# w_down as one DMA on 128 partitions and a fill tile ahead of the ring, in a decode kernel of cached attention and a gated feed-forward

## The chip, the cores and the metric

The kernel runs on one core of a Trainium2 chip. The metric is the device time of one execution in microseconds (us), the median of several runs; less is better.

## The reference

One token `x` of width 512 goes through two branches, and a scalar gate mixes them:

```python
g = sigmoid((x * gate_w).sum(-1, keepdims=True))
# a: attention of one query per head over a cache of 65536 keys; 32 heads of width 128
q = (x @ wq).reshape(B, Sq, H, Dh).transpose(0, 2, 1, 3)
scores = einsum("bhqd,bhkd->bhqk", q, k_cache) * Dh ** -0.5
o = einsum("bhqk,bhkd->bhqd", softmax(scores), v_cache)
a = o.transpose(0, 2, 1, 3).reshape(B, Sq, H * Dh) @ wo
# b: feed-forward of inner width 1792
b = (silu(x @ w_gate) * (x @ w_up)) @ w_down
out = g * a + (1 - g) * b
```

All tensors are bfloat16. K and V together are 1,073,741,824 bytes; w_down (1792 x 512) is 1,835,008 bytes, all other weights together some 12 MB.

## The kernel before

**Tiles and slots.** A head's K is cut into four tiles (`G = 4`), and so is its V, 128 tiles of each. A tile is 128 partitions x 128 rows x 128 bfloat16: 32,768 bytes in each partition, 4 MB, one DMA. The tiles live in a ring of five slots (`ring`, `SLOTS = 5`). `take` hands out the slot that has been free longest and `give` returns one; in the beginning the slots also hold the rest of wq (`wq_t`), w_gate and w_up (`gu_t`) and w_down (`wd_t`), and at the end the last half of wo (`wo_late`). Small tiles that stay for the whole kernel lie in `consts`, which is placed ahead of the ring in SBUF.

K0, K1, ... and V0, V1, ... below are the tiles by the number `n` of the code: K4 is K's fifth tile, the first of the second head.

**A tile of K.** VectorE multiplies it in place by the head's query (`products`, L254), then halves its width by adding (L258, once for the first head, twice after it). TensorE sums what is left over the width with an identity matrix (`scores`, L267), and VectorE adds up the last four columns (`fold`, L281). When a head's four tiles are through, the maximum and the exponentials follow (`row_max`, `exponentials`), and the weights of the sum go into `P_sb`.

**A tile of V.** TensorE multiplies it by the weights (`values`, L322, 32 matmuls a tile). V runs four tiles or more behind K. At the end of a head its result is turned, scaled and projected through wo (`head_copy`, `head_turn`, `project`).

**The order.** The program is scheduled by hand (`manual_schedule`): each engine runs its instructions in the order in which the code issues them. All large loads are issued by SyncE, in one queue. An issue waits until its slot has been released by the engine that read it last, and the issues behind it wait with it. Eight semaphores are used in turn for the DMAs, so that an issue also waits until the DMA eight places before it has landed.

**The beginning.** The order of the large loads is: the first columns of wq, K0, K1, K2, the rest of wq, w_gate, K3, w_up, then six DMAs of w_down (`load_wd`, L402), K4, two more of w_down, V0, K5, V1, K6, a piece of wo, V2, and so on in turns of V and K (L110). w_down takes the slot that K1 gives up, K4 the one of wq, V0 the one of K2, K5 the one of w_gate and w_up, V1 the one of K3, and K6 the one of w_down.

**w_down.** It lies on 64 partitions, 28 of its rows in each (`HP = 64`, `GT = 28`). Each of its eight DMAs fills eight partitions, every fourth one from a first partition on:

```python
firsts = (0, 1, 2, 3, 32, 33, 34, 35)
part = slice(firsts[i], firsts[i] + 29, 4)
nc.sync.dma_start(out=wd_sb[part], in_=wd_rows[part])
```

**The feed-forward branch.** `feed_forward_in` makes gate and up on 128 partitions, 14 values in each (L178), while the fourth tile of K is worked on. `feed_forward_mid` makes `hT`, 128 x 14, on VectorE in the step of K4, between its maximum and its second half. `feed_forward_out` follows on TensorE in the same step, ahead of V0's products: two small matmuls turn `hT` into 64 partitions x 28 (`h_ps`, L227), ScalarE copies them to `h2` (L231), 28 matmuls against w_down add up to `b_ps` (L233), ScalarE scales the result into `b_sb` (L236), and it opens the accumulators `a_ps` of the output (L238). Then w_down's slot is given back.

Of the kernel before, what the change touches and what calls it, by code (L numbers as in the profile page):

```python
# [8 lines left out]
ACT = mybir.ActivationFunctionType  # L9
ALU = mybir.AluOpType  # L10
AXIS = mybir.AxisListType
P = 128
# [21 lines left out]
def kernel(  # L34
# [14 lines left out]
    nc = tc.nc  # L49
    bf16 = mybir.dt.bfloat16  # L50
    f32 = mybir.dt.float32

    _, H, Sk, Dh = A_k_cache.shape
    D = A_x.shape[2]
    F = B_w_gate.shape[1]
    KT = D // P
    FT = F // P
# [7 lines left out]
    consts = ctx.enter_context(tc.tile_pool(name="consts", bufs=1))  # L65
# [7 lines left out]
    psum_m = ctx.enter_context(tc.tile_pool(name="psum_m", bufs=2, space=bass.MemoryType.PSUM))  # L73
# [7 lines left out]
    def take(name):  # L81
        slot = free.pop(0)
        held[name] = slot
        return ring.tile(
            [P, NB * Dh], bf16, name=name.split(".")[0], tag=f"slot{slot}"
        )

    def give(name):
        free.append(held.pop(name))

    xT = consts.tile([P, KT], bf16, name="xT")
    gwT = consts.tile([P, KT], bf16, name="gwT")
    with nc.allow_non_contiguous_dma(reason="small"):
# [19 lines left out]
    def load_k(n):  # L113
        load(K_tiles, A_k_cache, n, "K_t")
# [13 lines left out]
    ident_b = consts.tile([P, P], bf16, name="ident_b")  # L128
# [85 lines left out]
    def feed_forward_mid(gu_sb, eg):  # L214
        nc.vector.tensor_scalar_add(eg, eg, 1.0)
        nc.vector.reciprocal(eg, eg)
        hprod = consts.tile([P, FT], f32, name="hprod")
        nc.vector.tensor_tensor(out=hprod, in0=gu_sb[:, :FT], in1=eg, op=ALU.mult)
        hT = consts.tile([P, FT], bf16, name="hT")
        nc.vector.tensor_tensor(out=hT, in0=hprod, in1=gu_sb[:, FT:], op=ALU.mult)  # L220
        return hT

    def feed_forward_out(hT, rest):
        b_ps = psum_m.tile([1, D], f32, name="b_ps", tag="misc")
        h_ps = psum_m.tile([HP, GT], f32, name="h_ps", tag="misc")
        for r in range(2):
            nc.tensor.matmul(  # L227
                h_ps[:, r * FT : (r + 1) * FT], lhsT=ident_b[:, r::2], rhs=hT, start=True, stop=True
            )
        h2 = consts.tile([HP, GT], bf16, name="h2")  # L230
        nc.scalar.activation(out=h2, in_=h_ps, func=ACT.Copy)  # L231
        for t in range(GT):
            nc.tensor.matmul(  # L233
                b_ps, lhsT=h2[:, t : t + 1], rhs=wd_sb[:, t, :], start=(t == 0), stop=(t == GT - 1)
            )
        nc.scalar.activation(out=b_sb, in_=b_ps, func=ACT.Copy, scale=rest)  # L236
        for i, a in enumerate(a_ps):
            nc.tensor.matmul(  # L238
                a, lhsT=ones_f[0:1, 0:1], rhs=b_sb[:, i * HD : (i + 1) * HD], start=True, stop=False
            )  # L240
# [22 lines left out]
    def scores(n):  # L263
        S = F_tiles[n] = psum_s.tile([P, NB, QUAD], f32, name="S_ps")
        width = width_of(n)
        for c in range(0, width, QUAD):
            nc.tensor.matmul(  # L267
                S,
                lhsT=ident_b,
                rhs=K_tiles[n][:, :, c : c + QUAD],  # L270
                start=(c == 0),
                stop=(c == width - QUAD),
            )
        del K_tiles[n]
        give(f"K_t.{n}")
# [98 lines left out]
    def score_tile(n):  # L374
        for _ in products(n):
            pass
        if n:
            fold(n - 1)
# [11 lines left out]
    score_tile(1)  # L390
    xs = gate_sum()
    scores(1)
    wd_t = take("wd_t.0")
    HP = P // 2
    GT = F // HP
    wd_sb = wd_t[:HP, : GT * D].rearrange("p (t n) -> p t n", t=GT)
    wd_rows = B_w_down.rearrange("(p t) n -> p t n", t=GT)
    firsts = (0, 1, 2, 3, 32, 33, 34, 35)

    def load_wd(i):  # L400
        part = slice(firsts[i], firsts[i] + 29, 4)
        nc.sync.dma_start(out=wd_sb[part], in_=wd_rows[part])  # L402

    for i in range(6):
        load_wd(i)
    for g in range(1, H // QG):
        queries(g)
    give("wq_t.0")
    eg2 = gate_exp(xs)
    load_k(4)  # L410
    load_wd(6)
    load_wd(7)
    score_tile(2)
    rest = gate_value(eg2)
    scores(2)
# [17 lines left out]
    for n, v in steps:  # L433
# [22 lines left out]
        if n == G:  # L456
            hT = feed_forward_mid(*ff)
# [7 lines left out]
        if n == G:  # L465
            feed_forward_out(hT, rest)
            give("wd_t.0")
# [49 lines left out]
```

## Time and profile before

| | us |
|---|---|
| median of 3 runs | 2534.05 |
| lowest, highest run | 2532.77, 2534.06 |
| the profiled execution, its own time | 2534.41 |
| its span (first to last instruction) | 2532.6 |

| engine | busy us | share of the span |
|---|---|---|
| PE (TensorE matmuls) | 1533.7 | 61% |
| PEld (TensorE weight loads, beside the matmuls) | 581.6 | 23% |
| DVE (VectorE) | 2083.7 | 82% |
| ACT (ScalarE) | 77.7 | 3% |
| POOL (GpSimd) | 0.9 | 0% |

The profile is one execution. 1088.49 MB were moved by sixteen DMA engines, 430 GB/s over the span. In the profile's views PE, DVE, ACT, POOL and SP are the engines, a q behind the name is the engine's own queue in which it issues DMAs, L254 is line 254 of the kernel, and `out<-in` names the tile written and the tiles read. The chain of waits is followed back from the last instruction to whatever released each step. In the windows, a DMA's packet counts in the stretch in which it starts, so that shares of short stretches can be over 1.

### The profile page before, as it was taken

To read this page: it belongs to the slowest core of one execution; us is meant where nothing else is said; L and a number is where in the kernel's file an instruction comes from. 1 tells how busy PE (TensorE), PEld (TensorE's weight loads), DVE (VectorE), ACT (ScalarE), POOL (GpSimd) and SP (SyncE) were. 2 spreads that over 40 slices of the span, in tenths; PEclk is the share of its full clock that TensorE was granted. 3 is DMA by queue.
4 is the path that set the end of the run, shared out by engine and by line. 5 is a ranking of instruction groups with operands and counts; after the bars stand their busy time and mean duration, and the time that the engine had idled before them with its cause. 6 is when DMAs were issued, how large, how long until landed. Compare 5 with 4: busy or idle time off the path is not lost.

```text
span 2532.6 us, 13195 instructions
## 1 busy us (share of the span) xinstructions
PE 1533.7 (61%) x5786; PEld 581.6 (23%) x5786; DVE 2083.7 (82%) x744; ACT 77.7 (3%) x208; POOL 0.9 (0%) x7
## 2 busy tenths in 40 slices
PE   4656656665566555555665566556656665665569
PEld 1222222222222112222222122222222221222223
DVE  7788888888887999988888888888888888888860
ACT  1000000000000000000000000000000000000000
POOL 0000000000000000000000000000000000000000
PEclk9777777777777787787777777777777777777779
DMA  9999999999999999999999999999999999999998
GB/s 412 418 431 433 435 432 430 434 433 432 431 433 434 431 433 434 432 431 434 433 432 433 434 432 432 435 431 432 432 434 432 431 435 433 431 434 433 432 432 351
DMA packets 43915, 1088.49 MB, mean 430 GB/s; under 512 B 4753, under 2 KB 9362, under 8 KB 10258
## 3 DMA queue, kind: packets, MB, share of 16 engines
q1 hardware_dynamic: 43570, 1087.65, 99.7%
q8 instruction: 45, 0.74, 0.1%
q14 instruction: 12, 0.10, 0.0%
q10 hardware_dynamic: 288, 0.00, 0.0%
HBM read 1087.64 MB, written 0.00 MB: 429 GB/s over the span
## 4 chain that ended last, share of the span: by engine, by line
DMA 71%; PE 23%; DVE 4%; issue 1%; ACT 0%; SPq 0%; DVEq 0%
DMA V_t<-in_A_v_cache_dram 63%; PE O_ps L322 21%; DMA K_t<-in_A_k_cache_dram 8%; DVE K_t L254 3%; DVE K_t L258 1%; PE S_ps L267 1%; DMA wo_late<-in_A_wo_dram 0%; PE b_ps L233 0%; DVE S_sb L281 0%; DVE m L287 0%; PE oh_ps L351 0%; PE a_ps L238 0%; ACT P_sb L300 0%; PE a_ps L365 0%; PE mT_ps L291 0%
## 5 line engine op out<-in xcount | busy, mean ns | idle before, releaser
L322 PE MATMUL O_ps<-V_t,P_sb 128*4 128x512 bf16 x4094 | 1154.5, 452 | 663.5 <-DMA V_t<-in_A_v_cache_dram 663.5
L254 DVE TENSOR_TENSOR K_t<-K_t,q_bc 128x16384 bf16<-128x16384 bf16 (+1 forms) x159 | 1117.2, 7026 | 357.9 <-DMA K_t<-in_A_k_cache_dram 346.7
L258 DVE TENSOR_TENSOR K_t<-K_t 128x8192 bf16<-128x8192 bf16 (+1 forms) x314 | 859.7, 2738 | 8.6
L322 PEld LDWEIGHTS <-P_sb 128*4 128x4 bf16 x4094 | 393.0, 97 | 1405.1 <-issue 1064.1
L267 PE MATMUL S_ps<-K_t,ident_b 128*128 128x512 bf16 x1056 | 263.3, 393 | 100.6 <-DVE K_t L258 100.6
L267 PEld LDWEIGHTS <-ident_b 128*128 128x128 bf16 x1056 | 98.0, 101 | 248.0 <-issue 158.0
L291 PE MATMUL mT_ps<-diag,ones_f 128*128 128x128 f32 x64 | 24.5, 483 | 150.1 <-ACT diag L289 150.1
L351 PE MATMUL oh_ps<-ident_f,O_sb 4*128 4x1 f32 x256 | 55.5, 334 | 74.5 <-ACT O_sb L335 74.5
L281 DVE TENSOR_REDUCE S_sb<-S_ps 128x128 f32<-128x512 f32 x128 | 87.5, 683 | 4.9 <-PE S_ps L267 4.9
L289 ACT ACTIVATE diag<-ident_f,m 128x128 f32<-128x128 f32 x32 | 12.8, 401 | 2118.7 <-DVE m L287 2118.7
L351 PEld LDWEIGHTS oh_ps<-ident_f,O_sb 4*128 4x128 f32 x256 | 52.8, 301 | 84.1 <-ACT O_sb L335 82.9
L291 PEld LDWEIGHTS mT_ps<-diag,ones_f 128*128 128x128 f32 x64 | 15.2, 295 | 166.7 <-ACT diag L289 166.7
L484 DVE CAST out_sb<-a_ps 1x256 bf16<-1x256 f32 x1 | 0.4, 412 | 56.6 <-PE a_ps L365 56.6
L300 ACT ACTIVATE P_sb<-S_sb,bias 128x512 bf16<-128x512 f32 x32 | 23.1, 722 | 1.0
L287 DVE TENSOR_REDUCE m<-S_sb 128x1 f32<-128x512 f32 x32 | 22.0, 686 | 1.1
L335 ACT ACTIVATE O_sb<-O_ps 4x512 f32<-4x512 f32 x32 | 18.3, 572 | 129.2 <-PE O_ps L322 129.2
L313 DVE RECIPROCAL recip<-tot_ps 128x1 f32<-128x1 f32 x32 | 5.1, 158 | 13.0 <-PE tot_ps L308 13.0
L308 PEld LDWEIGHTS tot_ps<-rowsum,ones_f 128*128 128x128 f32 x64 | 9.5, 188 | 14.0 <-issue 14.0
L233 PE MATMUL b_ps<-wd_t,h 64*1 64x512 bf16 x28 | 12.1, 625 | 0.3 <-ACT h L231 0.3
L308 PE MATMUL tot_ps<-rowsum,ones_f 128*128 128x1 f32 x64 | 12.2, 260 | 0.0
L358 ACT ACTIVATE oT<-oh_ps,rg 128x1 bf16<-128x1 f32 x32 | 8.4, 263 | 65.0 <-PE oh_ps L351 65.0
L296 DVE TENSOR_REDUCE top<-mT_ps 128x1 f32<-128x128 f32 x32 | 9.1, 284 | 1.0 <-PE mT_ps L291 1.0
(47 smaller groups left out, 75.2 us busy)
## 6 DMA issues: line engine op xcount, KB each, us to landing
K_t<-in_A_k_cache_dram SPq DMA_DIRECT2D x128, 4096.0 KB, 35.3
V_t<-in_A_v_cache_dram SPq DMA_DIRECT2D x125, 4096.0 KB, 28.0
V_t<-in_A_v_cache_dram SPq DMA_DIRECT2D x4, 2048.0 KB, 31.1
wq_t<-in_A_wq_dram SPq DMA_DIRECT2D x1, 3584.0 KB
V_t<-in_A_v_cache_dram SPq DMA_DIRECT2D x3, 1024.0 KB
wo_sb<-in_A_wo_dram SPq DMA_DIRECT2D x4, 512.0 KB, 38.8
gu_t<-in_B_w_gate_dram SPq DMA_DIRECT2D x1, 1792.0 KB
gu_t<-in_B_w_up_dram SPq DMA_DIRECT2D x1, 1792.0 KB
```

Of the source, the lines that this page charges most:

```text
L254: yield nc.vector.tensor_tensor(out=K, in0=K, in1=q_rep, op=ALU.mult)
L258: yield nc.vector.tensor_tensor(out=K[:, :, 0:half], in0=K[:, :, 0:half], in1=K[:, :, half : 2 * half], op=ALU.add,)
L267: nc.tensor.matmul(S, lhsT=ident_b, rhs=K_tiles[n][:, :, c : c + QUAD], start=(c == 0), stop=(c == width - QUAD),)
L281: nc.vector.tensor_reduce(out=S_tiles[h][:, g * NB : (g + 1) * NB], in_=F_tiles.pop(n), axis=AXIS.X, op=ALU.add)
L287: nc.vector.tensor_reduce(out=m, in_=S_tiles[h], axis=AXIS.X, op=ALU.max)
L289: nc.scalar.activation(out=diag, in_=ident_f, func=ACT.Copy, scale=m)
L291: nc.tensor.matmul(mT_ps, lhsT=ones_f, rhs=diag, start=True, stop=True)
L300: nc.scalar.activation(out=P_tiles[h], in_=S_tiles[h], func=ACT.Exp, bias=bias, scale=scale, accum_out=rowsum[:, h : h + 1],)
L308: nc.tensor.matmul(tot_ps, lhsT=ones_f, rhs=rowsum[:, h : h + 1], start=True, stop=True)
L322: nc.tensor.matmul(O_tiles[h], lhsT=P_tiles[h][:, g * NB + j : g * NB + j + 4], rhs=V_tiles[n][:, j : j + 4, :], start=(g == 0 and j == 0) ...
L335: nc.scalar.activation(out=O_sb, in_=O_tiles.pop(h), func=ACT.Copy)
L351: nc.tensor.matmul(oh_ps, lhsT=O_sb[:, c * Dh : (c + 1) * Dh], rhs=ident_f[0:4, c : c + 1], start=(c == 0 and not turned), stop=(c == 3),)
```

## The change

There are two edits. A tile `fill` of 128 x 928 bfloat16, 1,856 bytes in each partition, which nothing reads or writes, is the first tile of `consts`; with it the five slots begin at 32,768, 65,536, 98,304, 131,072 and 163,840 bytes in the partition (before: 30,976 and each 32,768 further). And w_down comes on 128 partitions, 14 rows in each, as a single DMA, issued behind K4. It takes the slot of wq, and K4 the one of K1; K6 still takes the one that w_down gives back. `hT` is used as it is, so that the turning into 64 partitions is gone and 14 matmuls take the place of 28.

```diff
     def give(name):
         free.append(held.pop(name))
 
+
+    consts.tile([P, 928], bf16, name="fill")
     xT = consts.tile([P, KT], bf16, name="xT")
...
     def feed_forward_out(hT, rest):
         b_ps = psum_m.tile([1, D], f32, name="b_ps", tag="misc")
-        h_ps = psum_m.tile([HP, GT], f32, name="h_ps", tag="misc")
-        for r in range(2):
-            nc.tensor.matmul(
-                h_ps[:, r * FT : (r + 1) * FT], lhsT=ident_b[:, r::2], rhs=hT, start=True, stop=True
-            )
-        h2 = consts.tile([HP, GT], bf16, name="h2")
-        nc.scalar.activation(out=h2, in_=h_ps, func=ACT.Copy)
-        for t in range(GT):
-            nc.tensor.matmul(
-                b_ps, lhsT=h2[:, t : t + 1], rhs=wd_sb[:, t, :], start=(t == 0), stop=(t == GT - 1)
+        for t in range(FT):
+            nc.tensor.matmul(
+                b_ps, lhsT=hT[:, t : t + 1], rhs=wd_sb[:, t, :], start=(t == 0), stop=(t == FT - 1)
             )
...
     scores(1)
-    wd_t = take("wd_t.0")
-    HP = P // 2
-    GT = F // HP
-    wd_sb = wd_t[:HP, : GT * D].rearrange("p (t n) -> p t n", t=GT)
-    wd_rows = B_w_down.rearrange("(p t) n -> p t n", t=GT)
-    firsts = (0, 1, 2, 3, 32, 33, 34, 35)
-
-    def load_wd(i):
-        part = slice(firsts[i], firsts[i] + 29, 4)
-        nc.sync.dma_start(out=wd_sb[part], in_=wd_rows[part])
-
-    for i in range(6):
-        load_wd(i)
     for g in range(1, H // QG):
         queries(g)
     give("wq_t.0")
     eg2 = gate_exp(xs)
     load_k(4)
-    load_wd(6)
-    load_wd(7)
+    wd_t = take("wd_t.0")
+    wd_sb = wd_t[:, : FT * D].rearrange("p (t n) -> p t n", t=FT)
+    nc.sync.dma_start(out=wd_sb, in_=B_w_down.rearrange("(p t) n -> p t n", t=FT))
     score_tile(2)
```

## The prediction

> **What bounds the kernel now.** I read the page's chain first, then the slices, then the windows, and last the first 120 us in order of time. These are the page's slices, its DMA queues and its chain.
>
> ```profile
> DVE  7788888888887999988888888888888888888860
> DMA  9999999999999999999999999999999999999998
> GB/s 412 418 431 433 435 432 430 434 433 432 431 433 434 431 433 434 432 431 434 433 432 433 434 432 432 435 431 432 432 434 432 431 435 433 431 434 433 432 432 351
> ...
> q1 hardware_dynamic: 43570, 1087.65, 99.7%
> q8 instruction: 45, 0.74, 0.1%
> ...
> DMA 71%; PE 23%; DVE 4%; issue 1%; ACT 0%; SPq 0%; DVEq 0%
> ```
>
> The chain names DMA for 71%, and PE's 23% stands between two loads while the sixteen DMA engines go on working: they read 9 in every slice but the last. The windows say it more sharply (columns: stretch and its length, busy time of each engine with its instructions, granted clock, DMA share, GB/s).
>
> ```profile
> 60.00:78.00 18.00, 12.88 (x129) 8.74 (x127) 10.69 (x3) 0.41 (x2) 0.00 (x0) 0.72 1.03 444
> 78.00:96.00 18.00, 9.10 (x23) 2.96 (x24) 17.35 (x13) 1.60 (x5) 0.00 (x0) 0.52 1.01 436
> 96.00:98.00 2.00, 2.00 (x6) 0.61 (x5) 0.41 (x1) 0.00 (x0) 0.00 (x0) 0.50 0.68 295
> 98.00:100.00 2.00, 2.00 (x5) 0.37 (x3) 0.11 (x1) 0.00 (x0) 0.00 (x0) 0.50 0.88 377
> 100.00:102.00 2.00, 1.23 (x4) 0.33 (x4) 2.00 (x1) 0.68 (x1) 0.00 (x0) 0.50 1.13 393
> 102.00:104.00 2.00, 2.00 (x6) 0.47 (x5) 2.00 (x1) 0.00 (x0) 0.00 (x0) 0.50 0.66 279
> 104.00:2506.00 2402.00, 1458.79 (x5413) 548.55 (x5411) 2005.91 (x709) 67.31 (x186) 0.00 (x0) 0.77 1.00 433
> 2506.00:2510.00 4.00, 4.00 (x21) 1.55 (x19) 0.00 (x0) 0.00 (x0) 0.00 (x0) 1.00 0.97 410
> 2510.00:2514.00 4.00, 2.94 (x14) 1.08 (x13) 0.00 (x0) 0.00 (x0) 0.00 (x0) 1.00 0.96 391
> 2514.00:2518.00 4.00, 4.00 (x19) 1.61 (x19) 0.00 (x0) 0.00 (x0) 0.00 (x0) 1.00 0.96 368
> 2518.00:2522.00 4.00, 3.72 (x19) 1.36 (x17) 0.00 (x0) 0.00 (x0) 0.00 (x0) 1.00 0.55 202
> 2522.00:2526.00 4.00, 3.54 (x27) 1.84 (x25) 0.00 (x0) 0.59 (x1) 0.00 (x0) 1.00 0.75 228
> 2526.00:2530.00 4.00, 3.94 (x35) 2.83 (x35) 0.00 (x0) 0.26 (x1) 0.00 (x0) 1.00 0.07 25
> ```
>
> From 104 to 2506 us the share is 1.00: no engine runs dry. So a DMA engine that is behind at 104 us is still behind at the end, and the kernel ends when the latest of the sixteen has landed its last bytes. There are only two holes. Around 96 to 104 us the four shares miss 0.32 + 0.12 - 0.13 + 0.34, times 2 us: 1.30 us averaged over sixteen engines. At the end, the shares from 2506 to 2530 miss 0.03 + 0.04 + 0.04 + 0.45 + 0.25 + 0.93, times 4 us: 6.96 us. The end of the chain says when the last bytes came:
>
> ```profile
> 2516.42 12.18 DMA wo_late<-in_A_wo_dram
> 2528.60 0.04 issue
> 2528.65 1.48 PE a_ps L365 x12
> ```
>
> At 2528.60, 1.40 us before 2530. So the mean engine is done 6.96 - 1.40 = 5.56 us before the last one. That unevenness is what this change can touch.
>
> **Where the unevenness comes from.** One engine moves 433 / 16 = 27.06 GB/s; a K or V tile of 4,194,304 bytes is 262,144 bytes on each, 9.69 us. w_down is eight DMAs of 224 KB (229,376 bytes) on eight partitions each. The trace tells on how many engines one runs (first the timeline, with q for the queue that issues; then two rows of SyncE's waits).
>
> ```profile
> 46.38 4.19 SPq L402 DMA_DIRECT2D wd_t<-in_B_w_down_dram  x6
> 57.01 0.34 SPq L110 DMA_DIRECT2D K_t<-in_A_k_cache_dram  x1
> 62.34 1.71 SPq L402 DMA_DIRECT2D wd_t<-in_B_w_down_dram  x2
> 64.53 0.33 SPq L110 DMA_DIRECT2D V_t<-in_A_v_cache_dram  x1
> 66.84 0.33 SPq L110 DMA_DIRECT2D K_t<-in_A_k_cache_dram  x1
> 78.44 4.42 DVE L254 TENSOR_TENSOR K_t<-K_t,q_bc 128x8192 bf16<-128x8192 bf16 x1 [7.72 <-issue]
> 99.89 8.69 DVE L254 TENSOR_TENSOR K_t<-K_t,q_bc 128x16384 bf16<-128x16384 bf16 x1 [3.48 <-DMA K_t<-in_A_k_cache_dram]
> 100.10 0.33 SPq L110 DMA_DIRECT2D K_t<-in_A_k_cache_dram  x1
> ```
> ```profile
> SPq L402 <- DMA gu_t<-in_B_w_up_dram: 5.0, 1, 5.0
> SPq L110 <- PE b_ps L233: 19.5, 1, 19.5
> ```
>
> The seventh w_down DMA waited for w_up, so w_up had landed by 62.34; K's fifth tile is read from 78.44: 16.1 us for six w_down DMAs and a K tile. On eight engines, one row of 28,672 bytes each, six DMAs are 172,032 bytes, with the tile 434,176: 16.04 us. Spread over sixteen it would be 348,160 bytes: 12.87 us. The next step agrees: 78.44 to 99.89 is 21.45 us for two w_down DMAs, a V and a K tile; eight engines make 21.49, sixteen 20.43. So all of w_down goes through the same half: 229,376 bytes, 8.48 us, on each of eight engines and nothing on the others. I call them the loaded and the free half. The free half runs ahead and dries up at 96 to 104 us, because K's seventh tile waits for w_down's slot until the b_ps matmuls end (issue at 100.10). That hole, 1.30 x 16 / 8 = 2.6 us of each free engine, gives back part of the lag: about 8.48 - 2.6 = 5.9 us stay to the end (an estimate).
>
> **w_down as one DMA on 128 partitions.** It becomes 14,336 bytes in each of 128 partitions, the form of a K tile, which the tile's 9.69 us show on sixteen engines: 114,688 bytes each, 4.24 us. The loaded half has 8.48 - 4.24 = 4.24 us less to do. It never ran dry, so all of this comes off its end: **-4.24 us**. The free half takes 4.24 more and loses its hole of 2.6: +1.6 us.
>
> **The moves around it.** In SyncE's queue K's fifth tile now goes out when K's second tile's slot is free; w_down follows, waiting for wq's slot; behind it are V0, K5 and V1. These rows set the times:
>
> ```profile
> 46.18 6.20 PE L149 MATMUL qg_ps<-wq_t,X_bc 128*128 128x512 bf16 x28
> 59.98 6.83 PE L178 MATMUL gu_ps<-xT,gu_t 128*128 128x1 bf16 x112
> 70.17 6.07 PE L267 MATMUL S_ps<-K_t,ident_b 128*128 128x512 bf16 x16 [3.37 <-DVE K_t L258]
> 87.42 0.27 PE L227 MATMUL h_ps<-hT,ident_b 128*64 128x14 bf16 x2 [1.95 <-DVE hT L220]
> 87.97 12.10 PE L233 MATMUL b_ps<-wd_t,h 64*1 64x512 bf16 x28 [0.28 <-ACT h L231]
> 102.63 8.66 PE L322 MATMUL O_ps<-V_t,P_sb 128*4 128x512 bf16 x32
> ```
>
> K4 is issued at about 46.2 (before: 57.01), w_down at 52.4 when the queries end (before: 46 to 64), V0 when the third tile's scores are done, as gu_ps begins, about 60 (before 64.53, stuck behind the wait for w_up), K5 at 66.8 and V1 at 76.3 as before. The queue's work, from w_up's 62.34: K4 to 72.0, w_down 76.3, V0 86.0, K5 95.6, V1 105.3. Each issue is 9 us or more ahead of its turn, so the wait of w_down in SyncE's queue holds up nobody. VectorE reads K4 at 72.0 instead of 78.44; its first half ends after 76.24, when the fourth tile's scores are there to be folded, and hT follows 8.9 us after the start, as before (78.44 to 87.42): 80.9. PE's part: 28 matmuls of 12.10 / 28 = 0.43 us become 14, 6.05 us less; the two h_ps matmuls and the copy on ACT (87.42 to 87.97, 0.55 us) go. b_ps ends at 80.9 + 6.05 = 87.0, and K6, waiting for that slot, is issued there instead of at 100.10, 18 us before the queue is empty at 105.3. V2 follows when PE is through V0: 87.0, 2.6 for the steps between b_ps and O_ps (100.07 to 102.63), 8.66 of O_ps, 98.3, ahead of V1, K6 and a piece of wo. So the hole at 96 to 104 closes and no new one opens. PE's and VectorE's savings earn nothing of their own: they lie beside the transfers. If that cover were gone, K6 issued after 103 would cost all engines 1 us per us.
>
> **The fill.** It costs no instruction. In the built programs the slots move from 30,976 to 32,768 bytes in the partition (1,856 added, h2's 64 gone). No row shows a tile at another address, so I bound it. On VectorE:
>
> ```profile
> L254 DVE TENSOR_TENSOR K_t<-K_t,q_bc 128x16384 bf16<-128x16384 bf16 x97 | 843.1, 8691 | 264.9 <-DMA K_t<-in_A_k_cache_dram 261.5 <-DMA wo_sb<-in_A_wo_dram 3.4
> L254 DVE TENSOR_TENSOR K_t<-K_t,q_bc 128x8192 bf16<-128x8192 bf16 x62 | 274.1, 4421 | 93.0 <-DMA K_t<-in_A_k_cache_dram 85.3 <-issue 7.7
> ```
>
> Half tiles, of which the second begins 16,384 bytes further in, take half of a whole one, and VectorE idles 0.17 of 104 to 2506 us; a slower VectorE of a tenth would hide. On the DMA side the rate between slices runs from 430 to 435 GB/s at one set of addresses; a fill that moved the rate from 433 to either end would give 2402 x (433/435 - 1) = -11 us or 2402 x (433/430 - 1) = +17 us. I take 0, the value of the slots' equal slices, and keep both ends as rivals. The Trainium skill, "DMA: Bandwidth & Descriptors", section "How a descriptor splits into AXI transactions", says that only a start off a multiple of 256 bytes costs an extra transaction. 30,976 is 121 x 256, so by that rule the fill gains nothing. By that rule I give the end of -11 us less than the other.
>
> **The sum.** The profiled execution took 2534.41 us, 1.8 us more than its span of 2532.6; the median of the runs is 2534.05. 2534.41 - 4.24 = 2530.2, and against the median 2534.05 - 4.24 = **2529.8 us**. The gain's upper bound is perfect evenness: the last engine comes back to the mean, 5.56, and the mean has no hole, 1.30: 6.86 us, 2527.2. Its lower bound takes off the 1.3 us by which the runs differ: 2.9, 2531.1.
>
> **Rivals.**
> 1. *The last engine is one of the free half*, through something else than w_down, such as the 45 instruction packets of 16,384 bytes (0.61 us each at 27.06 GB/s). It would have to be 5.9 us behind its own half, ten packets more than its neighbours; 45 over sixteen engines are 2.8 each. Then the +1.6 us counts: 2535.7, no measurable change. Chance 0.10.
> 2. *The eight small DMAs cost time of their own.* Their issues take 4.19 + 1.71 = 5.9 us of SyncE, one takes some 0.4: 5.5 more, 2524.3. Against it: the share is 1.03 and 1.01 from 60 to 96 us, so the engines don't wait for SyncE. Chance 0.04. The Trainium skill, "SBUF — State Buffer", section "The DMA setup-cost knee", gives every transfer about 2 us that doesn't scale with bytes; seven fewer would be 14 us by it, and the trace disagrees where transfers queue behind each other.
> 3. *The fill raises the rate* to the best slice's: 2529.8 - 11 = 2518.8. Chance 0.05.
> 4. *The fill lowers the rate*, slower than before: at the worst slice's 430 GB/s 2529.8 + 17 = 2546.6. The rate decides from 0.37% down (431.4 GB/s; 4.24 + 5.07 us over some 2500) for slower by 0.2%. For it: every one of the 257 tiles is touched, and a round power of two is a new condition. Against it: the slots lie 32,768 bytes apart before and after, so how slots stand to each other doesn't change. Chance 0.11.
>
> **How the numbers follow.** The forecast's case has 0.70. A bound of 0.2%, 5.07 us, about what a measurement of this kernel can tell from no change, lies inside its range of gains, 2.9 to 6.9, near the middle: 0.32 of the 0.70 goes beyond it and 0.38 stays. Faster: 0.32 + 0.04 + 0.05 = 0.41. Same: 0.38 + 0.10 = 0.48. Slower: 0.11. The range takes in the forecast's case and rival 1, 0.80: 2527.1 to 2535.7.
>
> **What would show it.** In the profile after: K4 read by VectorE near 72 us without the 7.7 us of idling; 14 b_ps matmuls of 0.43 us; K6 issued near 87; shares at 1.0 from 96 to 104 us; 433 GB/s in the middle; and at the end a steeper fall of the share, with the last load 4 us earlier. Wrong it would be if a share under 1 stood anywhere before 2500 us, if the middle's rate were off 433 by 2 or more, or if the end came no earlier though the fall is steeper.

## The result, and the profile after

The changed kernel takes **2529.83 us** (median, 2529.58 to 2530.33 over 19 runs), the kernel before 2534.00 in the same comparison (2532.46 to 2535.21). The ratio is 0.9984, with a 95% interval of 0.9978 to 0.9990: 4.2 us less, 0.16%, clear of noise and inside the bound of 0.2%. The profiled execution took 2529.62 us with a span of 2527.8; that of before, 2534.41 and 2532.6. The two profiles are thus 4.8 us apart, 0.6 more than the medians. Of the 19 runs before, 15 lie at 2533.8 to 2534.5, three at 2532.5 to 2532.8 and one at 2535.2, while all 19 after lie within 0.8 us.

First the windows of the kernel after, with the same columns as before.

```profile
60.00:78.00 18.00, 12.04 (x130) 8.64 (x128) 16.40 (x7) 0.47 (x3) 0.00 (x0) 0.72 1.02 437
78.00:96.00 18.00, 14.59 (x55) 5.14 (x56) 12.21 (x11) 2.03 (x5) 0.00 (x0) 0.81 0.99 425
96.00:98.00 2.00, 1.79 (x9) 0.66 (x7) 2.00 (x1) 0.00 (x0) 0.00 (x0) 1.00 1.21 524
98.00:100.00 2.00, 0.00 (x0) 0.00 (x0) 2.00 (x1) 0.00 (x0) 0.00 (x0) 1.00 1.06 459
100.00:102.00 2.00, 0.00 (x0) 0.00 (x0) 2.00 (x1) 0.00 (x0) 0.00 (x0) 0.53 0.76 328
102.00:104.00 2.00, 0.00 (x0) 0.00 (x0) 2.00 (x1) 0.00 (x0) 0.00 (x0) 0.50 1.22 524
104.00:2506.00 2402.00, 1463.07 (x5395) 549.00 (x5395) 2001.85 (x709) 67.34 (x186) 0.00 (x0) 0.76 1.00 433
2506.00:2510.00 4.00, 2.76 (x13) 1.01 (x12) 0.00 (x0) 0.00 (x0) 0.00 (x0) 1.00 0.97 407
2510.00:2514.00 4.00, 4.00 (x20) 1.61 (x19) 0.00 (x0) 0.00 (x0) 0.00 (x0) 1.00 0.83 335
2514.00:2518.00 4.00, 3.76 (x19) 1.39 (x17) 0.00 (x0) 0.00 (x0) 0.00 (x0) 1.00 0.92 305
2518.00:2522.00 4.00, 3.54 (x29) 2.12 (x28) 0.00 (x0) 0.85 (x2) 0.00 (x0) 1.00 0.84 290
2522.00:2526.00 4.00, 3.38 (x30) 2.26 (x27) 0.41 (x1) 0.37 (x1) 0.00 (x0) 1.00 0.21 70
```

Three things are to be seen. The hole at 96 to 104 us is closed: the four shares average 1.06, before 0.84. The middle moves the same 433 GB/s at a share of 1.00. And at the end the shares stay at 0.83 or more until 2522 and then drop to 0.21; before, there was still 0.75 at 2522 to 2526.

The prediction named a share under 1 anywhere before 2500 us as a sign of being wrong. To the letter it is there (0.76 at 100 to 102 us, 0.99 at 78 to 96), but a stretch of 2 us counts a packet of 1.2 us where it starts. The transfers themselves leave no gap: V0, K5, V1 and K6 land on the first engine at 84.28, 93.96, 103.63 and 113.31 us, 9.7 us apart.

The first 100 us in order of time (the same lines of the code have other numbers here, because lines came and went):

```profile
53.00 0.33 SPq L395 DMA_DIRECT2D wd_t<-in_B_w_down_dram  x1
...
60.44 0.33 SPq L112 DMA_DIRECT2D V_t<-in_A_v_cache_dram  x1
...
67.10 0.33 SPq L112 DMA_DIRECT2D K_t<-in_A_k_cache_dram  x1
...
72.15 4.42 DVE L249 TENSOR_TENSOR K_t<-K_t,q_bc 128x8192 bf16<-128x8192 bf16 x1 [1.53 <-DMA K_t<-in_A_k_cache_dram]
75.07 0.33 SPq L112 DMA_DIRECT2D V_t<-in_A_v_cache_dram  x1
...
81.13 5.81 PE L228 MATMUL b_ps<-wd_t,hT 128*1 128x512 bf16 x14 [2.25 <-DVE hT L222]
...
86.97 0.33 SPq L112 DMA_DIRECT2D K_t<-in_A_k_cache_dram  x1
...
88.66 7.07 PE L317 MATMUL O_ps<-V_t,P_sb 128*4 128x512 bf16 x32
...
95.76 0.33 SPq L112 DMA_DIRECT2D V_t<-in_A_v_cache_dram  x1
```

VectorE reads K4 at 72.15 after 1.5 us of waiting, where it was 78.44 after 7.7; K6 is issued at 86.97 instead of 100.10. And the end of the chain:

```profile
2482.34 34.28 DMA V_t<-in_A_v_cache_dram
2516.63 0.04 issue
2516.67 3.19 PE O_ps L317 x14
...
2521.64 3.75 PE a_ps L360 x32
2525.39 0.02 issue
2525.42 0.37 ACT out_sb L468
```

The last wait is now for V's tail (the last pieces of V), which ends at 2516.63, and wo_late no longer stands in the chain; before, the last wait was for wo_late and ended at 2528.60. The two waits are not to be compared with each other, as the same rows of the kernel before show:

```profile
2521.35 3.18 PE L322 MATMUL O_ps<-V_t,P_sb 128*4 128x512 bf16 x14 [0.28 <-DMA V_t<-in_A_v_cache_dram]
...
2530.15 0.37 ACT L485 ACTIVATE out_sb<-a_ps 1x256 bf16<-1x256 f32 x1 [3.54 <-PE a_ps L365]
```

From these 14 matmuls on V's tail to the copy of the output it was 8.80 us before and is 8.75 after. The wait for wo_late was thus worth 0.05 us. What moved the end is V's tail, on which the matmuls start 4.68 us earlier (2521.35 and 2516.67).

Where the time came from is plainest in the trace's records of completion: a transfer on sixteen engines leaves sixteen of them, one when each engine is done. Before, w_down's eight DMAs leave eight each as they land, which shows directly what the prediction had worked out from times. The following rows are worked out from these records, in us behind the first engine, sorted (the bar marks the gap between the halves):

```
before, tile landing at 123.97 to 130.80:   0.0 0.1 0.1 0.1 0.1 0.2 0.2 0.3 | 5.1 5.2 5.2 5.2 5.2 5.5 6.2 6.8
after,  tile landing at 124.36 to 126.03:   0.0 0.0 0.0 0.0 0.0 0.0 0.1 0.1   0.2 0.2 0.3 0.3 0.4 1.1 1.6 1.7
before, tile landing at 2432.14 to 2446.09: 0.0 0.3 5.2 5.2 5.5 6.3 7.2 7.2   7.2 7.2 7.3 7.3 7.5 10.3 12.3 14.0
after,  tile landing at 2432.59 to 2441.35: 0.0 0.0 0.1 0.2 0.4 1.1 2.4 5.2   7.1 7.1 7.2 7.3 7.4 7.4 8.7 8.8
```

Before, eight engines are 5.1 us and more behind the other eight when the beginning is over. After, all sixteen leave the beginning within 1.7 us of each other. At the end the first engine lands 0.45 us later than before and the last one 4.74 us earlier.

The records do not say which engine is which, but the lags change so slowly from tile to tile that they can be followed through the run. No engine makes up more than 0.4 us of its lag in the 2300 us. Single engines fall back further, in steps of some 1.4 us: before, the last one in five steps from 6.8 to 14.0, and six of the free half from 0 to some 7.2.

### The profile page after: what moved, and what is told of

Its sections match the earlier page's. It is cut to its first block, busy times and chain, and to the rows that moved or that the text cites. A ratio compares the mean times of both kernels' runs of the same rounds, so it can differ in the third digit from the quotient of the medians.

```text
span 2527.8 us, 13150 instructions
## 1 busy us (share of the span) xinstructions
PE 1533.1 (61%) x5769; PEld 581.2 (23%) x5770; DVE 2083.8 (82%) x744; ACT 77.5 (3%) x207; POOL 0.9 (0%) x7
## 4 chain that ended last, share of the span: by engine, by line
DMA 72%; PE 23%; DVE 5%; issue 0%; ACT 0%; SPq 0%; DVEq 0%; ACTq 0%
DMA V_t<-in_A_v_cache_dram 65%; PE O_ps L317 22%; DMA K_t<-in_A_k_cache_dram 7%; DVE K_t L249 3%; DVE K_t L253 2%; PE S_ps L262 1%; DVE S_sb L276 0%; PE oh_ps L346 0%; PE a_ps L360 0%; DVE m L282 0%; ACT P_sb L295 0%; ACT O_sb L330 0%; PE mT_ps L286 0%; DVE top L291 0%; ACT diag L284 0%
## 5 line engine op out<-in xcount | busy, mean ns | idle before, releaser
L293 ACT ACTIVATE bias<-top 128x1 f32<-128x1 f32 x32 | 6.5, 203 | 62.8 <-DVE top L291 62.8
```

## The experiments

Four theories: **B**, the kernel ends with the DMA engine that has most bytes to move, and w_down's uneven split was the loss; **F**, the slots' address; **H**, the hole, that is K6's earlier issue; **N**, the number of DMAs. Each kernel was timed beside the kernel before, in five rounds unless the text says three; where it says so, it is a variant of the changed kernel.

### The fill: the change with the slots at 30,976

```diff
-    consts.tile([P, 928], bf16, name="fill")
+    consts.tile([P, 32], bf16, name="fill")
```

> The change with a fill of 64 bytes instead of 1,856: the slots begin at 30,976 as before the change, w_down comes as in the change. Theory B: 2529.8 us, all of the gain. Rival F (the round address brings it): 2534.0, or what part of it the address has.

2529.92 us, ratio 0.9984 (0.9975 to 0.9993). All of the gain is there at the old address: B.

### The fill alone

```diff
+    consts.tile([P, 896], bf16, name="fill")
     xT = consts.tile([P, KT], bf16, name="xT")
```

> The kernel before with a fill of 1,792 bytes alone: the slots begin at 32,768, w_down is as before in eight DMAs. Theory B: 2534.0 us, no change. Rival F: 2529.8, or less than 2534.0 by the address's part.

2534.05 us, ratio 0.9999 (0.9991 to 1.0008): at 32,768 the kernel before gains nothing. With the run ahead, 30,976 and 32,768 are the same, and F is out as a gain.

### The change without any fill

```diff
-    consts.tile([P, 928], bf16, name="fill")
```

> The change without its fill tile: w_down as one DMA on 128 partitions behind K4, h2 gone, so that the slots begin at 30,912 bytes in the partition. Theory B (bytes: the kernel ends with the DMA engine that has most left to move, and w_down's 4.24 us less on the loaded half are the whole gain): 2529.8 us, at 30,912 as at 32,768. Rival F (the fill, that is the slots' address, brings part or all of the gain): between 2529.8 and 2534.0. 30,912 is not a multiple of 256 (120.75 times), as 30,976 and 32,768 both are. The Trainium skill, DMA: Bandwidth & Descriptors, section How a descriptor splits into AXI transactions, gives a start off a multiple of 256 bytes an extra transaction of up to 8 beats; on a 32,768-byte row of 1,024 beats that would be up to 0.8%, some 20 us, by the page alone, and this run shows whether it holds on the SBUF side: 2530 if not, up to 2550 if so.

2540.10 us, ratio 1.0024 (1.0015 to 1.0034): 10.3 us slower than the change, and slower than before. The only difference to the first of these three kernels is 64 bytes of address. The window over the middle, first at 30,912, then at 30,976:

```profile
104.00:2500.00 2396.00, 1436.43 (x5321) 540.42 (x5320) 2002.53 (x709) 67.06 (x185) 0.00 (x0) 0.76 1.00 431
```
```profile
104.00:2500.00 2396.00, 1449.17 (x5369) 545.43 (x5369) 2001.94 (x709) 67.34 (x186) 0.00 (x0) 0.76 1.00 433
```

The engines are as busy, but 431 GB/s comes of it and not 433, the rate from which rival 4 was to decide. The mean packet of 32,768 bytes, over the 32,322 or so of 32,384 that took less than 1.4 us, takes 1216.9 ns there and 1213.1 at the other addresses. That is 0.32% more for a packet; the time grew by 0.41%, and the difference is not accounted for. So the fill does have a use in this change: taking `h2` out had moved the slots by 64 bytes, off a multiple of 256, and the fill puts them back on one.

### Another address off 256: 31,104

```diff
-    consts.tile([P, 928], bf16, name="fill")
+    consts.tile([P, 96], bf16, name="fill")
```

> The change with a fill of 192 bytes, so that the slots begin at 31,104 = 121.5 x 256 bytes; at 30,912 = 120.75 x 256 the same kernel took 2540.1, 10.3 us more than at 30,976 or 32,768. If what counts is a start at a multiple of 128 (or 64 would have done): 2529.8. If it is any start off a multiple of 256, at one price: 2540. If the price goes with the bytes from the 256 boundary to the start (192 there, 128 here): 10.3 x 128 / 192 = 6.9 more, 2536.7.

2539.73 us, ratio 1.0023 (1.0014 to 1.0032), a mean packet of 1217.1 ns. A start 128 bytes past a multiple of 256 costs 9.9 us, one 192 past 10.3: of the cases written down, one price for being off. Other distances were not tried. The Trainium skill, "DMA: Bandwidth & Descriptors", section "How a descriptor splits into AXI transactions", has that condition, a start off a multiple of 256 bytes. These runs agree with it for the side that writes SBUF, with 0.4% of the time, where up to 0.8% had been worked out from that page of the Trainium skill. They do not agree with the size that follows from its count of beats: by that section of the Trainium skill, as an estimate, 192 past would cost 6 beats of 1,024 and 128 past 4, and the two packets (1216.9 and 1217.1 ns) show no such difference.

### The hole: the kernel before with half of b_ps's sum

```diff
-        for t in range(GT):
-            nc.tensor.matmul(
-                b_ps, lhsT=h2[:, t : t + 1], rhs=wd_sb[:, t, :], start=(t == 0), stop=(t == GT - 1)
+        for t in range(FT):
+            nc.tensor.matmul(
+                b_ps, lhsT=h2[:, t : t + 1], rhs=wd_sb[:, t, :], start=(t == 0), stop=(t == FT - 1)
```

> The kernel before with 14 of the 28 matmuls of b_ps (half of the feed-forward sum is left out): K6 is issued 6 us earlier, at about 94 instead of 100.1, and nothing else changes. Theory B: the hole of the free half at 96 to 104 us closes wholly or nearly, and the time stays 2534.0, because the free half doesn't end last. Rival H (the gain came from closing that hole, by K6's earlier issue): the 1.3 us of the mean engine or the 2.6 us of the free half come off, 2531.4 to 2532.7.

2533.82 us, ratio 0.9998 (0.9989 to 1.0006). The timeline has K6 7 us earlier, and the window shows what became of the hole:

```profile
92.84 0.33 SPq L110 DMA_DIRECT2D K_t<-in_A_k_cache_dram  x1
```
```profile
96.00:104.00 8.00, 8.00 (x26) 2.65 (x25) 5.35 (x1) 0.00 (x0) 0.00 (x0) 0.67 0.94 406
```

A share of 0.94 instead of 0.84. In the completion records the halves are still 8.2 us apart when K6 and V2 have landed, where it was 5.8 and 5.1 with the hole: the free half ran further ahead and gained the kernel nothing that can be told from noise. H is out as the gain. A small part may be its own: in the records K6 follows V1 on the loaded half after 10.0 us in the kernel before and 9.7 in this one, so that the hole seems to have cost that half, too, some 0.3 us.

### The number of DMAs: the change with five

```diff
-    nc.sync.dma_start(out=wd_sb, in_=B_w_down.rearrange("(p t) n -> p t n", t=FT))
+    wd_rows = B_w_down.rearrange("(p t) n -> p t n", t=FT)
+    for t0, t1 in ((0, 3), (3, 6), (6, 9), (9, 12), (12, FT)):
+        nc.sync.dma_start(out=wd_sb[:, t0:t1, :], in_=wd_rows[:, t0:t1, :])
```

> The change with w_down in five DMAs of 3, 3, 3, 3 and 2 rows, each on 128 partitions: the same bytes on each of the sixteen engines, five DMAs instead of one, and five pieces in each partition instead of one. Theory B: 2529.8 us, the same as the change. Rival N (a DMA costs time of its own, so that eight becoming one is the gain of 4.2 us, 0.6 for each): four more are 2.4 us, 2532.2.

2530.18 us, ratio 0.9985 (0.9976 to 0.9994), 0.35 over the change and not 2.4. The pieces account for it: a packet of 32,768 bytes takes 1213 ns and one of 16,384 takes 611, so that 9 ns of a packet don't scale, and four more on each of an engine's eight partitions are 0.3 us. N is out.

### More bytes, on sixteen engines and on eight

Both are the change with 884,736 bytes more, once as six DMAs on 128 partitions, once as six on eight.

```diff
     load_v(0)
+    more = wd_t[:, FT * D : FT * D + 3456]
+    for i in range(6):
+        part = A_wo[144 * i : 144 * (i + 1), :].rearrange("r n -> (r n)").rearrange("(p f) -> p f", f=576)
+        nc.sync.dma_start(out=more[:, 576 * i : 576 * (i + 1)], in_=part)
```

> The change with 884,736 bytes more behind V0 that nothing reads, in six DMAs on 128 partitions, into the free part of w_down's slot: 55,296 bytes on each of sixteen engines, 2.04 us. Theory B: 2529.8 + 2.0 = 2531.9 us. Rival N: six DMAs at 0.6 us more on top, 2535.5. If extra bytes there are hidden: 2529.8.

```diff
     load_v(0)
+    more = wd_t[:, FT * D : FT * D + 9216]
+    rows = A_wo[:864, :].rearrange("r n -> (r n)").rearrange("(p f) -> p f", f=9216)
+    for i, first in enumerate((0, 1, 2, 3, 32, 33)):
+        nc.sync.dma_start(out=more[slice(first, first + 29, 4)], in_=rows[8 * i : 8 * (i + 1)])
```

> The change with the same 884,736 bytes more behind V0 that nothing reads, in six DMAs too, but of eight partitions each as w_down was before: 110,592 bytes on each of eight engines, 4.09 us, and nothing on the others. Theory B: 2529.8 + 4.1 = 2533.9 us, twice the cost of the same bytes on sixteen engines. If the total of bytes counts and not the engine: 2531.9, as with the same bytes on sixteen. In its profile the shares at the end fall off over a longer stretch than with the bytes on sixteen.

On sixteen 2532.31 us, 2.5 more than the change (2.04 of bytes, and 0.4 for 48 small packets of 9 ns on each engine); on eight 2533.80, 4.0 more, with 4.1 expected. Without the 0.4 for small packets, the same bytes cost about twice as much on half of the engines: B. The two differ by 1.5 us, which the interval of each ratio (0.9986 to 1.0004 and 0.9992 to 1.0009) doesn't set apart, but ten of the eleven runs on eight, 2533.67 and more, lie above all eleven on sixteen, 2532.08 to 2532.45. The windows of the end, first for sixteen, then for eight:

```profile
2514.00:2518.00 4.00, 4.00 (x20) 1.53 (x19) 0.00 (x0) 0.00 (x0) 0.00 (x0) 1.00 0.82 323
2518.00:2522.00 4.00, 3.75 (x18) 1.35 (x16) 0.00 (x0) 0.00 (x0) 0.00 (x0) 1.00 0.79 293
2522.00:2526.00 4.00, 3.54 (x37) 2.80 (x36) 0.00 (x0) 0.85 (x2) 0.00 (x0) 1.00 0.59 204
2526.00:2530.00 4.00, 1.79 (x15) 1.03 (x13) 0.41 (x1) 0.37 (x1) 0.00 (x0) 1.00 0.06 20
```
```profile
2514.00:2518.00 4.00, 4.00 (x20) 1.61 (x19) 0.00 (x0) 0.00 (x0) 0.00 (x0) 1.00 0.89 342
2518.00:2522.00 4.00, 3.70 (x18) 1.35 (x16) 0.00 (x0) 0.00 (x0) 0.00 (x0) 1.00 0.89 319
2522.00:2526.00 4.00, 2.90 (x28) 2.07 (x27) 0.00 (x0) 0.85 (x2) 0.00 (x0) 1.00 0.44 150
2526.00:2530.00 4.00, 3.37 (x18) 2.10 (x18) 0.00 (x0) 0.00 (x0) 0.00 (x0) 0.57 0.05 17
```

The shares don't show the longer stretch that I had expected: they sum to nearly the same. The extra lag stands in the records of the beginning: at some 127 us the loaded half with eight is 4.0 us behind its free half and 1.7 behind the engines of the run with sixteen, with 1.65 expected (4.09 - 2.04 - 0.4). At 2453 us the last engines of the two profiles are only 0.1 us apart, because the engine that ends last took four of the steps of 1.4 us there, and five with sixteen. The 2.6 us between the two spans (2530.6 and 2533.2) arise in wo_late at the very end; the profile with eight, 2535.00 us, is one of the two longest of its eleven runs. So it is the medians and the records of the beginning that speak for B here, and not the end of these two profiles.

### One DMA on the 64 partitions: the kernel before

```diff
-    firsts = (0, 1, 2, 3, 32, 33, 34, 35)
-
-    def load_wd(i):
-        part = slice(firsts[i], firsts[i] + 29, 4)
-        nc.sync.dma_start(out=wd_sb[part], in_=wd_rows[part])
-
-    for i in range(6):
-        load_wd(i)
+    nc.sync.dma_start(out=wd_sb, in_=wd_rows)
...
-    load_wd(6)
-    load_wd(7)
```

> The kernel before with w_down in the same 64 partitions, 28 rows each, but as one DMA in place of the first six and none later. It tells what binds the eight small DMAs to half of the engines. Theory B with the engines chosen by the DMA's shape (64 partitions go over sixteen engines, four each): the lag is gone, 2529.8 us. If the partition chooses the engine: the loaded half keeps its 8.48 us, 2534.0. The Trainium skill, SBUF - State Buffer, section Door 1: The DMA port swizzle, says that partitions 0 to 63 reach only eight of the sixteen ports; by that rule all sixteen engines would take 8.48 us, 2534.0 too, but with both halves alike, a share of 1 and half of the GB/s while w_down comes.

2535.66 us, ratio 1.0007 (0.9998 to 1.0016), 5.8 over the change. The window and the timeline:

```profile
60.00:78.00 18.00, 13.65 (x132) 9.03 (x129) 10.92 (x3) 0.41 (x2) 0.00 (x0) 0.72 1.02 313
```
```profile
81.59 4.42 DVE L254 TENSOR_TENSOR K_t<-K_t,q_bc 128x8192 bf16<-128x8192 bf16 x1 [10.63 <-issue]
```

The share is 1.02, so all engines work, and only 313 GB/s come of it, before 444. In the completion records K4 lands on all sixteen within 1.6 us: the DMA's shape chose sixteen engines, and the lag between halves is gone. But w_down took each of them about 9 us: a packet of 28,672 bytes takes 2.25 us, in the kernel before 1.06. That is the third of the cases written down. The Trainium skill, "SBUF — State Buffer", section "Door 1: The DMA port swizzle", lets partitions 0 to 63 reach half of the ports, and the trace agrees, 9 us against 8.48 by the halved rate. The time is 1.7 us over what that case gave; 1.0 of it is in the records, where w_down and K4 together land 19.2 us after w_up instead of 8.48 + 9.69, and the rest is open. So 64 partitions cost the late engines about the same either way; what pays is the whole width of 128.

### An uneven split on purpose: the change with 68 and 60 partitions

```diff
-    nc.sync.dma_start(out=wd_sb, in_=B_w_down.rearrange("(p t) n -> p t n", t=FT))
+    wd_rows = B_w_down.rearrange("(p t) n -> p t n", t=FT)
+    nc.sync.dma_start(out=wd_sb[:68], in_=wd_rows[:68])
+    nc.sync.dma_start(out=wd_sb[68:], in_=wd_rows[68:])
```

> The change with w_down as two DMAs, of 68 and of 60 partitions. The Trainium skill, DMA: Bandwidth & Descriptors, section Why a DMA increments its semaphore by 16 and not by 1, says that a DMA takes the largest number of engines up to 16 that divides its 68 or 60 partitions, counted from the lowest: 4 engines with 17 partitions each, and 15 with 4 each. By that, four engines get 17 x 14,336 bytes more than w_down's even share less what they save: 301,056 bytes, 11.1 us, in place of 4.24; eleven others 57,344 bytes, 2.1 us; one nothing. Theory B, if those four are among the engines that end early (in the profile of the change the last loads land on the engines over a stretch of 8.8 us): the late ones have 2.1 us less, 2527.7 us, better than the change. If the four are among the late ones: up to 6.9 us more, 2536.7. If w_down's shape doesn't choose engines: 2529.8.

2547.10 us, ratio 1.0052 (1.0039 to 1.0065), 17 more than the change and worse than every case written down.

```profile
78.00:96.00 18.00, 0.79 (x2) 0.52 (x3) 13.95 (x13) 1.42 (x4) 0.00 (x0) 0.51 0.97 223
```
```profile
96.01 4.15 PE L228 MATMUL b_ps<-wd_t,hT 128*1 128x512 bf16 x12 [14.80 <-DMA wd_t<-in_B_w_down_dram]
```

The 68 partitions did go over four engines and the 60 over fifteen: the transfers have four and fifteen records of completion, the last at 91.5 and at 95.9 us. But from 78 to 96 us all engines together move 223 GB/s at a share of 0.97, half of what they can: nearly every packet of a tile that starts between 74 and 94 us takes 2.0 to 2.9 us instead of 1.21. w_down arrives so late that b_ps waits for it until 96. My sum by bytes took 27.06 GB/s for each engine whatever the others do, and that doesn't hold when engines write to partitions in another arrangement than in whole tiles. That they meet at the same ports is likely after the run on 64 partitions, but it isn't shown here.

### The slack: K6 held back

Both are the change, timed in three rounds, with b_ps's matmuls repeated; `n` is 3 and 5.

```diff
-        for t in range(FT):
+        for t in [*range(FT)] * n:
```

> The change with the 14 b_ps matmuls made three times over (the last time counts): w_down's slot comes back some 12 us later and K6 is issued at about 99 instead of 87. Theory B with the slack of the prediction (the queue has work until about 105): 2529.8 us, nothing lost. Rival H (K6's issue is what sets the end): 12 us more, 2542.

> The change with the 14 b_ps matmuls made five times over (the last time counts): K6 is issued at about 110, 5 us after the queue has run empty, and its first bytes come some 2 us later. Theory B: all sixteen engines stand still for 5 to 7 us once, and the end moves by as much: 2535 to 2537 us. Rival H: 23 us more, 2553. If the early stretch doesn't count at all: 2529.8.

2529.93 and 2529.84 us: nothing is lost. The timeline and a window with five:

```profile
81.20 17.67 PE L228 MATMUL b_ps<-wd_t,hT 128*1 128x512 bf16 x70 [2.25 <-DVE hT L222]
...
98.91 0.33 SPq L112 DMA_DIRECT2D K_t<-in_A_k_cache_dram  x1
```
```profile
96.00:104.00 8.00, 7.23 (x34) 2.52 (x32) 8.00 (x1) 0.68 (x1) 0.00 (x0) 1.00 1.04 451
```

The dose was too small: 70 matmuls took 0.25 us each where I had counted 0.42, because the granted clock went from 0.50 to 1.00 between 85 and 87 us, some 5 us after the first of them. That PE was busy is not enough to explain it: in the kernel before, the 28 matmuls on 64 partitions keep PE busy from 88 to 100 us, and the clock stays at 0.50. K6 was issued at 98.9, inside the slack, and not at 110. So 12 us of K6's earliness are shown to be worth nothing; what it costs beyond 103 us stays open.

## Why the prediction was right

**The bound.** That an engine which "is behind at 104 us is still behind at the end" is shown by the completion records: 5.1 us between the halves at 124 us, and 5.2 to 5.5 still at 2432 between engines of the two that made few or no steps. That the kernel ends with the last bytes is right but for the tail: the end follows V's last piece by 8.8 us of PE's and ScalarE's work, and wo_late's bytes land beside it.

**The main term.** -4.24 us for the loaded half; the medians moved by 4.17, and the last engine's landing of a late tile by 4.74. Adding 4.09 us to eight engines gave 4.0, and 2.04 to sixteen gave 2.5 with its packets, so the term is the right one and not only of the right size. That the median came within 0.1 us of the forecast is closer than the account allows, and so in part luck: the records put the loaded half 4.6 us earlier at 124 us, 4.24 by its bytes and some 0.3 by the hole, which the prediction did not count, and the runs of the kernel before lie in groups some 1.4 us apart. w_down also moved behind K4, which no run tried by itself; on the first engine it lands 4.26 us after K4, its bytes' 4.24, so that the order leaves no time to explain.

**The free half.** +1.6 us was expected of its first engine, 0.45 was seen. The mis-sized term is the hole: 2.6 us read off the shares, 3.4 by the completion records (the lag fell from 8.5 to 5.1), which leaves 0.8. The shares show less of a hole than there is, because they count as busy the eight packets that start the free engines again at 101.2 to 101.9 us, and these take 1.6 to 2.3 us instead of 1.21, 0.9 more on average. It changed nothing, because that half doesn't end last.

**The moves.** K4 read at 72.15 (72.0 expected), w_down issued at 53.0 (52.4), V0 60.4 (60), K5 67.1 (66.8), V1 75.1 (76.3), b_ps in 5.81 (6.05), K6 at 86.97 (87.0), V2 at 95.8 (98.3). Off are V1, by 1.2 us, and V2, by 2.5: the steps between b_ps and O_ps took 1.7 us instead of 2.6, and O_ps 7.07 instead of 8.66, at a granted clock of 1.00 where it had 0.81 before.

**The fill.** Taken at 0 between the two addresses, and 0 it is. Rivals 3 and 4 looked at whether 32,768 is better or worse than 30,976. Neither asked what stands at the address that the change would have without the fill. Rival 4's mechanism is real (a rate of 431, slower than before by 0.24%), only at another address, and the fill is what keeps the change clear of it.

**Rival 1** (the last engine in the free half) is not what the completion records show: followed back from tile to tile, the last three, at 10.3, 12.3 and 14.0, belong to the loaded half. But it was priced too low. A step is 1.4 us and not the 0.61 of an instruction packet's bytes, and by 2432 us six engines of the free half have fallen back by more than the 5.1 us that they were ahead. The loaded half still ends last because it falls back in the same steps. **Rival 2** fell with the five DMAs.

**The size against 0.2%.** The gain came a third of the way up its range, 2.9 to 6.9. The upper end was read too low: the shares put the mean engine 5.56 us ahead of the last, the records 7.1 before and 4.4 after (at 2432 us). The unevenness that is left, 8.8 us between first and last, grows slowly over the run, in steps of about 1.4 us on single engines at the times of the page's 45 instruction packets. In both kernels the last engine takes five of them, some 466 us or eight packets apart. That the packets cause the steps is likely, and also that the groups of times before, some 1.4 us apart, differ by one step of the last engine, but no run took the packets away.

## What to carry to other kernels

Where transfers bind a kernel from end to end, count bytes per DMA engine, not bytes in all: what one engine gets too much in the first 100 us, it is still late by 2400 us later. A short hole in the queue of the other engines makes the lag look smaller and costs next to nothing. A load on 128 partitions that divide like the big tiles is both even and at full rate; one on 64, on 8 at a time, or on 68 and 60 was not. And an edit that adds or removes a small tile moves every tile behind it, so look where the large ones then begin.

## What the runs showed of the hardware that I had not expected

- Slots that begin 128 or 192 bytes past a multiple of 256 cost 9.9 and 10.3 us of 2530 against 30,976 and 32,768, which are the same: 1217 instead of 1213 ns for a packet of 32,768 bytes.
- Single DMA engines fell back in steps of 1.4 us, and none made up more than 0.4 us of a lag in 2300 us: 1.7 us between first and last at 124 us became 8.8 at 2432.
- 28 matmuls on 64 partitions kept PE busy for 12 us at a granted clock of 0.50; 70 on 128 partitions had 1.00 after some 5 us.
- Sixteen engines that bring 64 partitions move 313 GB/s averaged over 18 us in which w_down's 1.8 MB came along, where eight engines on w_down beside eight on the next tile moved 444.
- Two DMAs of 68 and 60 partitions halved the rate of all transfers for some 18 us (223 GB/s at a share of 0.97).
